# One-core linear attention and two gated feed-forward layers: loop attention placed between the front products, one block's exponentials per head, gate halves on one engine

## The chip, the cores and the metric

The kernel runs on one core of one Trainium2 chip. The metric is the device time of one execution in microseconds, as the median of several runs. PE is the matrix engine, DVE the vector engine, ACT the scalar (activation) engine, POOL the GpSimd engine, SP the engine that issues the DMAs.

## What is computed

Attention without a score matrix, then two feed-forward layers, all in float32:

```python
# q, k, v: (8, 8, 576, 64)
q_s = softmax of q over the 64 head columns
k_s = softmax of k over the 576 positions
x = q_s @ (k_s^T @ v)                  # laid out as 4608 tokens x 512
x = ((sigmoid(x @ w_gate) * (x @ w_val)) @ w_out)       # 512 -> 1536 -> 512
h = x @ w_in                                            # 512 -> 2048
g = (a0 + a1*h + a2*h^2 + a3*h^3) / (1 + |b0|*|h| + |b1|*h^2 + 1e-6)
out = g @ w_out2                                        # 2048 -> 512
```

## The kernel before

Every large product is made of three matmuls of split operands: each float32 value is cut into a high half (rounded to the matmul's format, copied by ACT) and a low half (value minus high half, on DVE or POOL). `mm3` (L168 to L171) multiplies high by high, low by high and high by low. Weights arrive as 64-bit numbers and are turned into float32 by four DVE operations on their bits (`prep_bits_a`, `prep_bits_b`, L203 to L218) before they are split.

The 4608 tokens are worked off in 9 blocks `j` of 512. In the first layer a block has 12 steps `f` (one per 128 columns of the 1536). A step is: the front products `pg` and `pv` (`front_a`, 4 pieces `kk` of 6 matmuls each, 24 in all), the sigmoid of `pg` on ACT, its product with `pv` on DVE, the split of that gate into `gh` and `gl` (`vec_a`), and the back products of the step before (`back_a`, 12 matmuls). The tiles `pg` and `pv` of a step fill the pool `ps_f`, so the next step's `pg` waits for this step's sigmoid and its `pv` for this step's gate product.

Attention is done in units `(j, u)`, one per block and pair of heads. For k: the column maximum (`att_km`), a transpose `ps_kt`, a maximum `mx` and a copy on DVE, a transpose back `ps_kb`, a copy `kma` on ACT (`att_kt`, `att_kb`), a subtraction on POOL (`att_ks`), an exponential on ACT (`att_ke`), the product `ps_kv` with v. For q: maximum, subtraction, exponential, sum, reciprocal and product (`att_qm`, `att_qs`, `att_qe`, `att_n`), four transposes `ps_qt` (`att_q`). The last product `ps_xt` gives a piece of x (`att_d`). All of these PE results go through the two banks of the pool `ps_x`, in turn.

The order of the work has two regimes. Block 0 with the attention of blocks 0 and 1 and all weights of the first layer is ordered by a planner (`in_time`, L59 on): a table of costs per kind of operation (`KINDS`) decides which operation is issued next and, for kinds with two engines, whether it goes to DVE or POOL (`Chosen`, recorded at L472). From block 1 on, a loop (L606 to L632) issues the steps, and the attention of block `j` runs during block `j - 1`: unit `u` has a due step `d`, and its parts are issued at `d - 5` to `d`. Before the change a step issues them in three places: `early_work` (the transpose `ps_kt`) right after the front products, `work` beside the gate's split, and `late_work` (`ps_kb`, the k subtraction) after the back products. In the same loop `prep` converts the weights of the second layer and stores them in DRAM. Engines run their instructions in issue order.

The second layer (144 steps of a front product `ph`, some DVE and ACT work and a back product `accb`) follows, and the diff leaves it alone.

Of the kernel before, what the change touches and what calls it, by code (L numbers as in the profile page):

```python
# [10 lines left out]
F32 = mybir.dt.float32  # L11
# [8 lines left out]
P = 128  # L20
# [23 lines left out]
    "q_max": (DVE, 0.68), "q_sub": ({DVE: 0.7, POOL: 1.05},), "q_exp": (ACT, 0.63, "exp"),  # L44
# [7 lines left out]
    "front": (PE, 1.37), "sig": (ACT, 0.6, "sigmoid"), "gate": (DVE, 0.7), "g_h": (ACT, 0.63),  # L52
    "g_l": ({DVE: 0.7, POOL: 1.29},),
    "back": (PE, 2.73), "next_h": (ACT, 0.62), "next_l": ({DVE: 0.7, POOL: 1.29},),
# [64 lines left out]
def kernel(ctx: ExitStack, tc: tile.TileContext, q, k, v, w1, w2, ab_in, out):  # L119
# [15 lines left out]
    def f32(ap):  # L135
        return ap.bitcast(F32)
# [6 lines left out]
    exp_bias = const.tile([P, 1], F32, name="exp_bias")  # L143
    q_one = 1.0 + 1e-6
# [77 lines left out]
    def prep_split(p, eng=nc.gpsimd):  # L222
        if p < NW1:
            wt[p] = [wpool.tile([P, NB], F32R, tag="w", name=n) for n in ("wh", "wl")]
            yield from split_steps(*wt[p], val.pop(p), eng)
        else:
            hl = stage.tile([P, 2, NB], F32R, tag="raw", name="hl")
            yield from split_steps(hl[:, 0], hl[:, 1], val.pop(p), nc.gpsimd)
            yield
            nc.sync.dma_start(out=w2_d[p - NW1], in_=f32(hl))  # L230
# [6 lines left out]
    def prep(stage_of):  # L237

        for p, n in stage_of:
            yield from (prep_load, prep_abs, prep_bits_a, prep_bits_b, prep_split)[n](p) or ()  # L240
            yield
# [25 lines left out]
    kt, vt, qt, kmt, qm = {}, {}, {}, {}, {}  # L267
# [14 lines left out]
    def heads(t):  # L282
        return t.rearrange("p c (h d) -> p (c h) d", d=D)
# [25 lines left out]
    def att_qm(j, u):  # L309
        qm[j, u] = att.tile([P, 8], F32, tag="qm", name="qm", bufs=4)  # L310
        nc.vector.tensor_reduce(out=qm[j, u], in_=heads(qt[j, u]), axis=AX.X, op=ALU.max)
# [6 lines left out]
    def att_qe(j, u):  # L318
        nc.scalar.activation(qt[j, u], qt[j, u], AF.Exp)

# [8 lines left out]
    def att_n(j, u, eng):  # L329
        g = heads(qt[j, u])  # L330
        t = att.tile([P, 8], F32, tag="qs", name="qs")
        nc.vector.tensor_reduce(out=t, in_=g, axis=AX.X, op=ALU.add)
        yield
        nc.vector.tensor_scalar(out=t, in0=t, scalar1=1e-9, scalar2=None, op0=ALU.add)
# [116 lines left out]
    def op(name, emit, *after):  # L451
        ops[name] = emit, [a for a in after if a]
# [22 lines left out]
    for i in range(2 * NHP):  # L475
        j, u = divmod(i, NHP)

        def n(what, back=0):
            return (what, *divmod(i - back, NHP)) if i >= back else None
# [11 lines left out]
        op(n("q_max"), partial(att_qm, j, u), n("load_q"), n("q_max", 1), n("q_sub", 3))  # L491
        op(n("q_sub"), partial(att_qs, j, u, Chosen(n("q_sub"))), n("q_max"))
        op(n("q_exp"), partial(att_qe, j, u), n("q_sub"))
        op(n("k_exp"), partial(att_ke, j, u), n("k_sub"), j and n("q_exp"))
        chain([n("q_sum"), n("q_add"), n("q_inv"), n("q_div")], att_n(j, u, Chosen(n("q_div"))), n("q_exp"), n("q_sum", 1), n("q_div", 2))
# [65 lines left out]
    work, early_work, late_work = {}, {}, {}  # L561

    def at(step, fn, *args):
        work.setdefault(max(step, NF1), []).append((fn, args))

    for j in range(2, NBLK):
        for u in range(NHP):
            d = NF1 * (j - 1) + UNIT_STEPS[u]
            if (j, u) != (2, 0):
                at(d - 5, load_k, j, u) if j < B else None  # L570
                at(d - 5, load_q, j, u)
# [12 lines left out]
            at(d - 1, att_q, j, u)  # L584
            at(d, att_d, j, u)
# [11 lines left out]

    prep_at = {}
    for p in range(NW1, NW):
        at0 = NF1 + 2 + 5 * (p - NW1) // 2  # L600
        for n, step in enumerate((0, 1, 1, 2, 2)):
            prep_at.setdefault(at0 + step, []).append((p, n))
# [176 lines left out]
```

## Time and profile before

| what | value |
|---|---|
| median of 3 runs | 1834.7 us (1833.99 to 1836.22) |
| the profiled execution, its own time | 1834.72 us |
| its span, first to last instruction | 1832.9 us |
| mean granted PE clock | 0.992 of full speed |
| PE, DVE, ACT, POOL busy, share of the span | 97%, 65%, 55%, 20% |
| HBM read, written | 92.44 MB, 35.65 MB |

The busy share is an average. PE's idle time lies in the first 850 us of the span; what it waits for there differs between the planned block and the loop, so they are read apart. A time in a row is in microseconds from the span's start unless it is a mean in ns.

### The profile page before, as it was taken

The numbers are of one execution on the slowest core, as the hardware profiler recorded it, in microseconds if no ns is written. First come the engines' busy times: TensorE is split into PE (matmuls) and PEld (weight loads), VectorE is DVE, ScalarE is ACT, GpSimd is POOL, SyncE is SP. The second block draws the span as 40 slices with busy tenths as digits, with TensorE's granted clock in tenths as the row PEclk, the third lists the DMA queues.
The fourth block names the chain that finished last, engine by engine and source line by source line (L and its number), as shares of the span: only waits on it lengthen the run. The fifth ranks groups of instructions, "written<-read, shape, count | busy, mean of one in ns | idle before, by whom it ended". The sixth has DMA issues, their size and how long they took to land.

```text
span 1832.9 us, 22295 instructions
## 1 busy us (share of the span) xinstructions
PE 1772.1 (97%) x8384; PEld 1452.7 (79%) x8384; DVE 1182.3 (65%) x1925; ACT 1005.6 (55%) x1652; POOL 363.3 (20%) x279
## 2 busy tenths in 40 slices
PE   5988999999999999999999999999999999999999
PEld 3766787787888878778888888888888888888887
DVE  9998545445455454454430288888888888887876
ACT  4556443444435354443331387777676777777765
POOL 3543010101011010110001122222222222222222
PEclk7999999999999999999999999999999999999999
DMA  6442323223132321312226401010000000000000
GB/s 206 146 150 89 115 68 107 69 64 114 62 123 75 110 79 54 123 61 84 78 77 212 160 24 43 5 47 12 35 23 24 24 24 24 23 24 24 1 24 23
DMA packets 53388, 129.54 MB, mean 71 GB/s; under 512 B 5664, under 2 KB 5664, under 8 KB 53280
## 3 DMA queue, kind: packets, MB, share of 16 engines
q1 hardware_dynamic: 53280, 128.12, 21.0%
q8 instruction: 66, 1.08, 0.2%
q14 instruction: 42, 0.34, 0.1%
HBM read 92.44 MB, written 35.65 MB: 70 GB/s over the span
## 4 chain that ended last, share of the span: by engine, by line
PE 56%; DVE 0%; ACT 0%; issue 0%
PE accb L698 21%; PE ph L171 7%; PE ph L170 7%; PE ph L169 7%; PE acc L430 4%; PE pg L169 1%; PE pv L169 1%; PE pg L171 1%; PE pv L171 1%; PE pg L170 1%; PE pv L170 1%; PE ps_qt L372 0%; PE ps_xt L170 0%; PE ps_xt L169 0%; PE ps_xt L171 0%; DVE km L287 0%
## 5 line engine op out<-in xcount | busy, mean ns | idle before, releaser
L415 DVE TENSOR_TENSOR sg<-pv,sg 128x512 f32<-128x512 f32 x108 | 74.4, 689 | 375.7 <-ACT sg L413 208.1
L162 POOL TENSOR_TENSOR glb<-gb,ghb 128x512 fp32r<-128x512 f32 x144 | 187.3, 1301 | 604.1 <-ACT ghb L160 585.4
L413 ACT ACTIVATE sg<-pg 128x512 f32<-128x512 f32 x108 | 64.5, 597 | 388.8 <-PE pg L171 387.0
L666 ACT ACTIVATE h<-ph 128x512 f32<-128x512 f32 x144 | 86.1, 598 | 196.9 <-PE ph L171 196.8
L169 PE MATMUL pg<-x_h,wh 128*128 128x512 f32 x432 | 172.1, 398 | 1.9 <-ACT sg L413 1.9
L169 PE MATMUL pv<-x_h,wh 128*128 128x512 f32 x432 | 169.3, 392 | 2.0 <-DVE sg L415 2.0
L170 PE MATMUL pv<-x_h,wl 128*128 128x512 f32 x432 | 168.9, 391 | 0.3 <-DVE wl L472 0.3
L171 PE MATMUL pv<-x_l,wh 128*128 128x512 f32 x432 | 168.9, 391 | 0.0
L170 PE MATMUL pg<-x_h,wl 128*128 128x512 f32 x432 | 168.8, 391 | 0.0
L171 PE MATMUL pg<-x_l,wh 128*128 128x512 f32 x432 | 168.7, 391 | 0.0
L698 PE MATMUL accb<-wh,ghb 128*128 128x512 f32 x576 | 158.3, 389 | 0.0
L698 PE MATMUL accb<-wl,ghb 128*128 128x512 f32 x576 | 158.3, 389 | 0.0
L698 PE MATMUL accb<-wh,glb 128*128 128x512 f32 x576 | 158.3, 389 | 0.0
L669 DVE SCALAR_TENSOR_TENSOR ah<-h,babs,ah 128x512 f32<-128x512 f32 x144 | 107.9, 750 | 54.5 <-ACT ah L667 54.5
L162 POOL TENSOR_TENSOR hl<-val,hl 128x512 fp32r<-128x512 f32 x32 | 41.3, 1290 | 475.1 <-ACT hl L160 224.3
L430 PE MATMUL acc<-gh,wl 128*128 128x512 f32 x432 | 122.4, 395 | 5.0 <-POOL wl L472 5.0
L430 PE MATMUL acc<-gh,wh 128*128 128x512 f32 x432 | 125.9, 402 | 0.4 <-DVE x_raw L436 0.3
L698 PEld LDWEIGHTS accb<-wl,ghb 128*128 128x128 f32 x576 | 108.1, 188 | 22.5
L698 PEld LDWEIGHTS accb<-wh,glb 128*128 128x128 f32 x576 | 108.1, 188 | 22.4
L698 PEld LDWEIGHTS accb<-wh,ghb 128*128 128x128 f32 x576 | 108.1, 188 | 22.4
L685 DVE SCALAR_TENSOR_TENSOR u<-ah,r 128x512 f32<-128x512 f32 x144 | 99.3, 690 | 39.5 <-ACT r L675 39.5
L169 PE MATMUL ph<-x_h,wh 128*128 128x512 f32 x320 | 124.5, 389 | 0.0
(129 smaller groups left out, 3974.5 us busy)
## 6 DMA issues: line engine op xcount, KB each, us to landing
raw<-in_w SPq DMA_DIRECT2D x68, 512.0 KB, 4.6
w<-hl SPq DMA_DIRECT2D x32, 512.0 KB, 2.9
v<-in_v SPq DMA_DIRECT2D x30, 325.0 KB, 3.3
k<-in_k SPq DMA_DIRECT2D x30, 320.0 KB, 4.1
q<-in_q SPq DMA_DIRECT2D x36, 256.0 KB, 4.2
x<-x_raw SPq DMA_DIRECT2D x36, 256.0 KB, 2.3
x_raw<-x SPq DMA_DIRECT2D x9, 1024.0 KB, 5.4
out<-ob SPq DMA_DIRECT2D x36, 256.0 KB, 2.3
```

Of the source, the lines that this page charges most:

```text
L162: lo_eng.tensor_tensor(out=lo, in0=src, in1=f32(h), op=ALU.subtract)
L169: nc.tensor.matmul(ps, wh, xh, start=first, stop=False)
L170: nc.tensor.matmul(ps, wl, xh, start=False, stop=False)
L171: nc.tensor.matmul(ps, wh, xl, start=False, stop=last)
L413: nc.scalar.activation(sg, pg, AF.Sigmoid)
L415: nc.vector.tensor_tensor(out=sg, in0=pv, in1=sg, op=ALU.mult)
L430: nc.tensor.matmul(accs["a", j][m], x[:, m * P:(m + 1) * P], y, start=(f == 0 and n == 0), stop=(f == NF1 - 1 and n == 2))
L666: nc.scalar.activation(h2, ph, AF.Square)
L669: nc.vector.scalar_tensor_tensor(out=ah, in0=h2, scalar=babs[:, 1:2], in1=ah, op0=ALU.mult, op1=ALU.add)
L685: nc.vector.scalar_tensor_tensor(out=u, in0=ah, scalar=q_one, in1=r, op0=ALU.add, op1=ALU.mult)
L698: nc.tensor.matmul(accs["b", j][t], x[:, t * P:(t + 1) * P], y, start=(f == 0 and n == 0), stop=(f == NF2 - 1 and n == 2))
```

## The change

1. **Loop attention.** The three lists of a step become one, keyed by step and by the piece `kk` of the front products after which the work is issued. `ps_kt`, `mx` and the copy come after piece 0 of step `d - 3`, `ps_kb`, `kma` and the k subtraction after piece 1, `ps_kv` and `ps_qt` after piece 2 of step `d - 1`, `ps_xt` after piece 0 of step `d`. The q exponential moves from step `d - 2` (next to the k exponential) to step `d - 3`, the q maximum and subtraction from `d - 4` to `d - 3`.
2. **Block 1's q exponential** (in the planned part) is done per head on ACT: eight activations of 128x64 that take the negated maximum as bias and write the row sums. Its subtraction and its sum on DVE or POOL fall away.
3. **Low halves.** In the planner's table `g_l` and `next_l` are DVE only.
4. The constant 1e-9 of the q sum comes from a tile `eps`; the store of a converted weight is issued one step after its split.

```diff
-    "q_max": (DVE, 0.68), "q_sub": ({DVE: 0.7, POOL: 1.05},), "q_exp": (ACT, 0.63, "exp"),
+    "q_max": (DVE, 0.68), "q_sub": ({DVE: 0.7, POOL: 1.05},), "q_exp": (ACT, 0.63, "exp"), "q_exps": (ACT, 2.1, "exp"),
...
-    "g_l": ({DVE: 0.7, POOL: 1.29},),
-    "back": (PE, 2.73), "next_h": (ACT, 0.62), "next_l": ({DVE: 0.7, POOL: 1.29},),
+    "front": (PE, 1.37), "sig": (ACT, 0.6, "sigmoid"), "gate": (DVE, 0.7), "g_h": (ACT, 0.63), "g_l": (DVE, 0.7),
+    "back": (PE, 2.73), "next_h": (ACT, 0.62), "next_l": (DVE, 0.7),
...
-            nc.sync.dma_start(out=w2_d[p - NW1], in_=f32(hl))
+            val[p] = hl
+
+    def prep_store(p):
+        nc.sync.dma_start(out=w2_d[p - NW1], in_=f32(val.pop(p)))
...
+    def att_qf(j, u):
+        g, m = heads(qt[j, u]), qm.pop((j, u))
+        qs[j, u] = att.tile([P, 8], F32, tag="qs", name="qs")
+        for i in range(8):
+            s = slice(i, i + 1)
+            nc.scalar.activation(g[:, i, :], g[:, i, :], AF.Exp, bias=m[:, s], accum_out=qs[j, u][:, s])
+            if i % 4 == 3:
+                yield
...
-                at(d - 4, att_km, j, u)
-                early_work.setdefault(max(d - 3, NF1 + 1), []).append((att_kt, (j, u, ps_x, "x")))
-                late_work.setdefault(max(d - 3, NF1 + 1), []).append((att_kb, (j, u, ps_x, "x")))
-                late_work[max(d - 3, NF1 + 1)].append((att_ks, (j, u, nc.gpsimd)))
-                at(d - 2, att_ke, j, u)
-                at(d - 3, load_v, j, u)
-                at(d - 1, att_kv, j, u)
-            at(d - 4, att_qm, j, u)
-            at(d - 4, att_qs, j, u, nc.vector)
-            at(d - 2, att_qe, j, u)
-            at(d - 2, att_n, j, u, nc.vector)
-            at(d - 1, att_q, j, u)
-            at(d, att_d, j, u)
+                at(d - 4, 1, att_km, j, u)
+                at(d - 3, 0, att_kt, j, u, ps_x, "x")
+                at(d - 3, 1, att_kb, j, u, ps_x, "x")
+                at(d - 3, 1, att_ks, j, u, nc.gpsimd)
+                at(d - 3, 2, load_v, j, u)
+                at(d - 2, 0, att_ke, j, u)
+                at(d - 1, 2, att_kv, j, u)
+            at(d - 3, 0, att_qm, j, u)
+            at(d - 3, 0, att_qs, j, u, nc.vector)
+            at(d - 3, 1, att_qe, j, u)
+            at(d - 2, 0, att_n, j, u, nc.vector)
+            at(d - 1, 2, att_q, j, u)
+            at(d, 0, att_d, j, u)
...
         for kk in range(KC):
             front_a(f, kk, *ps)
+            run(sequence((), work.get((i, kk), [])))
...
-        run(sequence((), early_work.get(i, [])))
-        run(prep(prep_at.get(i, [])), sequence(vec, work.get(i, [])))
+        run(vec, prep(prep_at.get(i, [])))
         if pend:
             back_a(*pend.pop(0))
-        run(sequence((), late_work.get(i, [])))
```

How the order moves at three places that the prediction speaks of.

PE, in a loop step of kind `d - 3` (the first unit of a block; `ps_kt` and `ps_kb` are the two transposes, `acc` the back products, `pg` and `pv` the front products). Before:

```order
L171 MATMUL pv<-x_l,wh 128x512
L293 MATMUL ps_kt<-ident,km 128x128
L430 MATMUL acc<-gh,wh 128x512 x4
L430 MATMUL acc<-gh,wl 128x512 x4
L430 MATMUL acc<-gl,wh 128x512 x4
L303 MATMUL ps_kb<-ident,km 128x128
```

and with the change:

```order
L172 MATMUL pv<-x_l,wh 128x512
L296 MATMUL ps_kt<-ident,km 128x128
L170 MATMUL pg<-x_h,wh 128x512
L171 MATMUL pg<-x_h,wl 128x512
L172 MATMUL pg<-x_l,wh 128x512
L170 MATMUL pv<-x_h,wh 128x512
L171 MATMUL pv<-x_h,wl 128x512
L172 MATMUL pv<-x_l,wh 128x512
L306 MATMUL ps_kb<-ident,km 128x128
```

The pair of transposes has moved from the two ends of the back products into the front products, six matmuls apart.

ACT, in a loop step that has the k transposes of one unit and the products of the unit before it (`kvh` and `qh` are the copies of `ps_kv` and `ps_qt`, `sg` the sigmoid, `gh` the gate's high half, ACT_TABLE_LOAD the change between the tables of exponential and sigmoid). Before:

```order
L413 ACTIVATE sg<-pg 128x512
L160 ACTIVATE gh<-sg 128x512
L360 ACTIVATE kvh_93<-ps_kv,rs 64x64 x2
L377 ACTIVATE qh<-ps_qt 128x512
L306 ACTIVATE kma<-ps_kb 128x128
```

and with the change:

```order
L309 ACTIVATE kma<-ps_kb 128x128
L322 ACT_TABLE_LOAD
L322 ACTIVATE q<-q 128x512
L375 ACTIVATE kvh_95<-ps_kv,rs 64x64 x2
L392 ACTIVATE qh<-ps_qt 128x512
L428 ACT_TABLE_LOAD
L428 ACTIVATE sg<-pg 128x512
L161 ACTIVATE gh<-sg 128x512
```

The step's sigmoid now stands behind a q exponential, two table loads and the copies of the attention products. Over the whole program the table loads go from 67 to 119.

POOL, in the planned block (`wl` are low halves of weights, `gl` of gates, `q` and `k` subtractions and products of the attention). A middle piece before:

```order
L472 TENSOR_TENSOR q<-q,qm 128x512
L472 TENSOR_TENSOR gl<-sg,gh 128x512
L472 TENSOR_TENSOR wl<-early,wh 128x512
L472 TENSOR_TENSOR gl<-sg,gh 128x512
L472 TENSOR_TENSOR wl<-early,wh 128x512 x2
L472 TENSOR_TENSOR gl<-sg,gh 128x512
```

and with the change:

```order
L487 TENSOR_TENSOR wl<-early,wh 128x512
L487 TENSOR_TENSOR q<-q,qs 128x512
L487 TENSOR_TENSOR wl<-early,wh 128x512 x13
L487 TENSOR_TENSOR q<-q,qs 128x512
L487 TENSOR_TENSOR k<-k,kma 128x640
```

In the planned block POOL's operations go from 46 to 33: `gl` 10 to 0, `wl` 23 to 20, the q subtraction 5 to 3, the k subtraction 6 to 5, the q product 2 to 5. On DVE `gl` goes from 2 to 12, `wl` from 13 to 16, the k subtraction from 2 to 3, the q subtraction from 3 to 1, the q product from 6 to 3, the q sum from 8 to 4.

## Rows read from the trace of the kernel before

**Rows 1.** Busy time by stage: stretch, length, busy us and count per engine, clock, DMA.

```profile
50.00:175.00 125.00, 106.53 (x511) 82.31 (x509) 119.06 (x194) 73.53 (x124) 65.25 (x36) 0.96 0.42 136
175.00:850.00 675.00, 658.25 (x3394) 539.55 (x3393) 326.68 (x634) 285.29 (x484) 74.03 (x52) 1.00 0.26 86
850.00:1800.00 950.00, 950.00 (x4199) 786.43 (x4198) 670.27 (x979) 606.74 (x975) 199.78 (x154) 1.00 0.13 45
```

**Rows 2.** Waits of PE from 175 to 850 us: total us, times, longest.

```profile
PE ps_qt L372 <- DVE mx L296: 12.3, 18, 1.1
PE ps_kb L303 <- DVE kvl L364: 3.7, 7, 1.2
```

**Rows 3.** PE in order of time in one loop step: start, us, what [idle before].

```profile
315.96 0.33 PE L293 MATMUL ps_kt<-ident,km 128*128 128x128 f32 x1
316.22 0.80 PE L348 MATMUL ps_kv<-v,k 128*64 128x65 f32 x20
318.17 0.63 PE L372 MATMUL ps_qt<-ident,q 128*128 128x128 f32 x4 [1.15 <-DVE mx L296]
...
322.76 0.30 PE L303 MATMUL ps_kb<-ident,km 128*128 128x128 f32 x1 [1.19 <-DVE kvl L364]
```

**Rows 4.** DVE in order of time in the same step.

```profile
317.15 0.68 DVE L415 TENSOR_TENSOR sg<-pv,sg 128x512 f32<-128x512 f32 x1
317.75 0.28 DVE L296 TENSOR_REDUCE mx<-ps_kt 128x1 f32<-128x128 f32 x1
318.06 0.23 DVE L298 COPY km<-mx 128x128 f32<-128x128 f32 x1
```

**Rows 5.** DVE in order of time in the planned block.

```profile
107.75 1.78 DVE L218 SCALAR_TENSOR_TENSOR early<-raw,early 128x512 uint32<-128x512 uint32 x1
```

**Rows 6.** POOL in order of time at the same place.

```profile
107.30 1.68 POOL L472 TENSOR_TENSOR gl<-sg,gh 128x512 fp32r<-128x512 f32 x1 [1.90 <-ACT gh L160]
```

**Rows 7.** Groups by line: `early` planned block, `val` loop; xcount, busy us, mean ns, idle.

```profile
L215 DVE SCALAR_TENSOR_TENSOR early<-raw,early 128x512 uint32<-128x512 uint32 x34 | 31.8, 935 | 0.0
...
L218 DVE SCALAR_TENSOR_TENSOR early<-raw,early 128x512 uint32<-128x512 uint32 x34 | 30.5, 898 | 0.0
...
L218 DVE SCALAR_TENSOR_TENSOR val<-raw,val 128x512 uint32<-128x512 uint32 x34 | 23.5, 692 | 1.1
L215 DVE SCALAR_TENSOR_TENSOR val<-raw,val 128x512 uint32<-128x512 uint32 x34 | 23.2, 683 | 0.0
...
L205 DVE TENSOR_SCALAR early<-early 128x512 f32<-128x512 f32 x34 | 20.6, 613 | 0.3 <-ACT early L199 0.2
...
L208 DVE TENSOR_SCALAR early<-early 128x512 uint32<-128x512 uint32 x34 | 19.8, 582 | 0.0
...
L208 DVE TENSOR_SCALAR val<-val 128x512 uint32<-128x512 uint32 x34 | 15.7, 462 | 0.1
L205 DVE TENSOR_SCALAR val<-val 128x512 f32<-128x512 f32 x34 | 14.5, 427 | 11.8 <-ACT val L199 11.6
```

**Rows 8.** Line L472 (operations with an engine chosen by the planner) by stage.

```profile
0.00:175.00 175.00, 21.80 (x28) 79.67 (x46) 0.91 0.47 154
```

**Rows 9.** Group by line of ACT: the table loads that precede a sigmoid.

```profile
L413 ACT ACT_TABLE_LOAD x33 | 42.3, 1283 | 5.5 <-PE pg L171 4.9
```

**Rows 10.** ACT in order of time in two loop steps.

```profile
331.69 1.28 ACT L327 ACT_TABLE_LOAD   x1
332.99 0.74 ACT L327 ACTIVATE k<-k 128x640 f32<-128x640 f32 x1
333.63 0.61 ACT L319 ACTIVATE q<-q 128x512 f32<-128x512 f32 x1
334.26 1.28 ACT L413 ACT_TABLE_LOAD   x1
...
341.00 0.63 ACT L360 ACTIVATE kvh<-ps_kv,rs 64x64 fp32r<-64x64 f32 x2 [1.09 <-DVE rs L355]
341.66 0.60 ACT L377 ACTIVATE qh<-ps_qt 128x512 fp32r<-128x512 f32 x1
```

More of the change, by code (lines that the diff above doesn't have):

```diff
@@ L51 @@
     "w_h": (ACT, 0.62), "w_l": ({DVE: 0.7, POOL: 1.29},),
-    "front": (PE, 1.37), "sig": (ACT, 0.6, "sigmoid"), "gate": (DVE, 0.7), "g_h": (ACT, 0.63),
-    "g_l": ({DVE: 0.7, POOL: 1.29},),
-    "back": (PE, 2.73), "next_h": (ACT, 0.62), "next_l": ({DVE: 0.7, POOL: 1.29},),
+    "front": (PE, 1.37), "sig": (ACT, 0.6, "sigmoid"), "gate": (DVE, 0.7), "g_h": (ACT, 0.63), "g_l": (DVE, 0.7),
+    "back": (PE, 2.73), "next_h": (ACT, 0.62), "next_l": (DVE, 0.7),
 }
@@ L143 @@
     exp_bias = const.tile([P, 1], F32, name="exp_bias")
+    eps = const.tile([P, 8], F32, name="eps")
+    nc.vector.memset(eps, 1e-9)
     q_one = 1.0 + 1e-6
@@ L228, in prep_split @@
             yield from split_steps(hl[:, 0], hl[:, 1], val.pop(p), nc.gpsimd)
-            yield
-            nc.sync.dma_start(out=w2_d[p - NW1], in_=f32(hl))
+            val[p] = hl
+    def prep_store(p):
+        nc.sync.dma_start(out=w2_d[p - NW1], in_=f32(val.pop(p)))
     def fetch(p):
@@ L239, in prep @@
         for p, n in stage_of:
-            yield from (prep_load, prep_abs, prep_bits_a, prep_bits_b, prep_split)[n](p) or ()
+            yield from (prep_load, prep_abs, prep_bits_a, prep_bits_b, prep_split, prep_store)[n](p) or ()
             yield
@@ L266 @@
     att = att_ctx.enter_context(tc.tile_pool(name="att", bufs=2))
-    kt, vt, qt, kmt, qm = {}, {}, {}, {}, {}
+    kt, vt, qt, kmt, qm, qs = {}, {}, {}, {}, {}, {}
     def load_k(j, u):
@@ L307, in att_kb, with att_qm @@
         yield
-    def att_qm(j, u):
+    def att_qm(j, u, negate=False):
         qm[j, u] = att.tile([P, 8], F32, tag="qm", name="qm", bufs=4)
-        nc.vector.tensor_reduce(out=qm[j, u], in_=heads(qt[j, u]), axis=AX.X, op=ALU.max)
+        nc.vector.tensor_reduce(out=qm[j, u], in_=heads(qt[j, u]), axis=AX.X, op=ALU.max, negate=negate)
     def att_qs(j, u, eng):
@@ L330, in att_n @@
         g = heads(qt[j, u])
[L331 to L334, printed above, removed]
+        t = qs.pop((j, u), None)
+        if t is None:
+            t = att.tile([P, 8], F32, tag="qs", name="qs")
+            nc.vector.tensor_reduce(out=t, in_=g, axis=AX.X, op=ALU.add)
+            yield
+        nc.vector.tensor_tensor(out=t, in0=t, in1=eps, op=ALU.add)
         yield
@@ L490 @@
         op(n("k_sub"), partial(att_ks, j, u, Chosen(n("k_sub"))), n("k_cp"))
-        op(n("q_max"), partial(att_qm, j, u), n("load_q"), n("q_max", 1), n("q_sub", 3))
-        op(n("q_sub"), partial(att_qs, j, u, Chosen(n("q_sub"))), n("q_max"))
-        op(n("q_exp"), partial(att_qe, j, u), n("q_sub"))
+        op(n("q_max"), partial(att_qm, j, u, j == 1), n("load_q"), n("q_max", 1), n("q_exp", 3))
+        if j == 0:
+            op(n("q_sub"), partial(att_qs, j, u, Chosen(n("q_sub"))), n("q_max"))
+            op(n("q_exp"), partial(att_qe, j, u), n("q_sub"))
+        else:
+            op(n("q_exps"), lambda g=att_qf(j, u): next(g), n("q_max"), n("q_div", 2), n("q_exp", 1))
+            op(n("q_exp"), ops[n("q_exps")][0], n("q_exps"))
         op(n("k_exp"), partial(att_ke, j, u), n("k_sub"), j and n("q_exp"))
-        chain([n("q_sum"), n("q_add"), n("q_inv"), n("q_div")], att_n(j, u, Chosen(n("q_div"))), n("q_exp"), n("q_sum", 1), n("q_div", 2))
+        chain(([] if j else [n("q_sum")]) + [n("q_add"), n("q_inv"), n("q_div")],
+              att_n(j, u, Chosen(n("q_div"))), n("q_exp"), n("q_add", 1), n("q_div", 2))
         chain([n("kv"), n("kv_add"), n("kv_inv"), n("kv_h"), n("kv_l")], att_kv(j, u), n("k_exp"), n("load_v"))
@@ L559, with at @@
         ops[o][0]()
-    work, early_work, late_work = {}, {}, {}
-    def at(step, fn, *args):
-        work.setdefault(max(step, NF1), []).append((fn, args))
+    work = {}
+    def at(step, kk, fn, *args):
+        work.setdefault((step, kk) if step >= NF1 else (NF1, 0), []).append((fn, args))
     for j in range(2, NBLK):
@@ L569 @@
             if (j, u) != (2, 0):
[L570 to L571 removed]
+                at(d - 5, 2, load_k, j, u) if j < B else None
+                at(d - 5, 2, load_q, j, u)
             if j < B:
[L573 to L585 removed]
+                at(d - 4, 1, att_km, j, u)
[11 more added lines that the diff above has]
+            at(d, 0, att_d, j, u)
     def split_x():
@@ L600 @@
         at0 = NF1 + 2 + 5 * (p - NW1) // 2
-        for n, step in enumerate((0, 1, 1, 2, 2)):
+        for n, step in enumerate((0, 1, 1, 2, 2, 3)):
             prep_at.setdefault(at0 + step, []).append((p, n))
```

## The prediction, made before the changed kernel was run

> **What bounds the kernel now.** I read the busy time by stage first [rows 1]. From 850 to 1800 us PE is busy for the whole 950 us: the second layer, which the change doesn't touch, and nothing can be won there. 950 us for 4199 matmuls is 0.226 us each, the pace of PE when it never waits. Two stages remain. In the loop (175 to 850 us) PE is busy 658.25 of 675 us, so 16.75 us idle. In the planned block it is DVE that is full: from 50 to 175 us DVE works 119.06 of 125 us, PE 106.53, ACT 73.53 [rows 1]. A gain has to come from one of these two: from PE's waits in the loop, or from DVE's work in the planned block.
>
> The waits of PE in the loop are two [rows 2]: 12.3 us in 18 waits of `ps_qt` for the reduction `mx`, and 3.7 us in 7 waits of `ps_kb` for `kvl`. One step shows the first [rows 3]: `ps_kt` starts at 315.96, `ps_kv` follows, and `ps_qt`, which needs the bank of `ps_kt`, waits 1.15 us. DVE reads that bank late [rows 4]: `mx` comes after the gate product of the step, which starts at 317.15, so it starts at 317.75. The back products are queued behind that `ps_qt` on PE. The second wait is the mirror image: `ps_kb` stands after the back products and needs the bank of `ps_kv`, which `kvl` leaves late (1.19 us). Neither is a shortage of an engine: DVE works 326.68 of the 675 us. PE waits because four users of two banks stand close together and DVE reaches them behind other work.
>
> **The change, part by part.**
>
> *The loop.* Now six front matmuls (6 x 0.226 = 1.36 us) stand between `ps_kt` and `ps_kb`, six more before `ps_kv` and `ps_qt`, and the bank of `ps_kt` has been read long before. `mx` and the copy take 0.28 + 0.23 us [rows 4], with 0.33 us of `ps_kt` before them [rows 3] and some 0.1 us of handing on (`mx` ends at 318.03, `ps_qt` starts at 318.17) about 0.95 us, under the 1.36 us of cover. In issue order `mx` now has ahead of it only the previous step's gate work, which falls into that step's back products (12 x 0.226 = 2.71 us) and the first piece. So both waits should go: 16.0 us [rows 2], and 16.75 us as the bound of what is idle. Against it: where `ps_kt`, `ps_kv` and `ps_qt` were one group, they are now two. The small matmuls take 0.26 us from `ps_kt` to the next start against 0.226 for a full product [rows 3], so one more break per unit costs PE at most some 0.1 us, 24 units 2.4 us, at least nothing. I take **-15 us**. The bound on the gainful side is -18: the idle time and 1.25 us from transposes that now overlap products. On the other side it is -8, half of the waits replaced by new ones.
>
> The price of the move lies on ACT. The q exponential had shared a table with the k exponential of the same step: load, k, q, load [rows 10]. One step earlier it needs its own pair of loads: 24 units x 2 loads x 1.283 us [rows 9] = 62 us more on ACT, which is busy 285.29 of 675 us [rows 1]. That is 2.6 us more in a step of nearly 10 us. I cost it at nothing because ACT waits for PE there; if that cover goes, the sigmoid is late, and next step's `pg` on PE with it. I work the slack out in the second rival.
>
> The k loads keep their step but the maximum that reads them comes earlier in its step; the weight stores leave their old place, where SP stood waiting for POOL with the next loads queued behind, so SP is relieved. Both beside other work: nothing.
>
> *The planned block.* DVE gains 10 gate halves, 3 weight halves and one k subtraction, and loses 2 q subtractions, 3 q products and 4 q sums. At 0.68 us for 128x512, as the gate product [rows 4], the k subtraction 640/512 of it, that is (10 + 3 + 1.25 - 2 - 3 - 4) x 0.68 = **+3.6 us**. That looks like a loss, since DVE is the full engine. But POOL's operations are not free for DVE. [rows 5] and [rows 6] show a DVE operation of 1.78 us while POOL's operation runs from 107.30 to 108.98; the same line takes 0.69 us in the loop [rows 7]. The four bit operations average 935, 898, 613 and 582 ns in the planned block against 683, 692, 427 and 462 ns in the loop [rows 7]: 0.76 us per weight, 34 weights, 26 us. POOL issues 46 operations there [rows 8], so 0.57 us of DVE each. The change takes 13 of them away: -7.4 us. The balance is 3.6 - 7.4 = -3.8 us. I take **-4 us**, as DVE is the full engine and PE stands in its shadow. The bounds: if each of the 13 had cost the full 1.78 - 0.68 = 1.10 us, -14.3 + 3.6 = -10.7; if the remaining 33 block DVE as often as the 46 did, +3.6.
>
> The Trainium skill, page "SBUF — State Buffer", section "SBUF: two separate sides", says that DVE and GpSimd share one port pair under an exclusive lock, held for a whole instruction, and that a DVE operation with two SBUF inputs is among those that block. By that rule every POOL operation that meets such work costs its full length, and the sum would go to the -10.7 end; the trace's average of 0.57 us says that about half of them meet it.
>
> The per-head exponentials replace 4 activations of 0.61 us [rows 10] by 32 small ones. No row shows one with row sums. The nearest from below is a `kvh` copy of 64 columns with a per-partition scalar, 0.31 us (two take 0.63 [rows 10]); from above, the whole exponential, 0.61. So +7.5 to +17 us of ACT, and four table loads more in this stage, 5.1 us. ACT goes from 73.53 to between 86 and 96 of the 125 us: not yet full, so nothing, which holds as long as DVE is the later one.
>
> The constant `eps` and the halves `next_l` (on DVE before too) change nothing.
>
> **The sum.** -15 - 4 = -19 us. The profiled execution took 1834.72 us (span 1832.9 and 1.8 around it), the median is 1834.7, so the sum goes straight onto it: **1815.7 us**.
>
> **The rivals.**
>
> *The planned block does not get shorter.* Were DVE blocked as often as before, or the planner's new order worse, the +3.6 us stays: 1834.7 - 15 + 3.6 = 1823.3. For it: what blocks DVE is when a POOL operation falls, and ACT's 12 to 22 us more can hold up a weight copy that DVE waits for. Against it: 13 fewer operations are certain. Chance 0.20.
>
> *The sigmoid comes late (slower).* In a step with `ps_kv`, count from its start. `ps_kv` 0.80 [rows 3], DVE's sum and reciprocal with their handing on some 0.4 (an estimate: the small DVE copy takes 0.23 [rows 4]), the two `kvh` 0.63, `qh` 0.60 [rows 10], the load 1.28, the sigmoid 0.60: it ends about 4.5 us after. PE goes through `ps_kv` and `ps_qt` (0.80 + 0.39), six front matmuls (1.36) and twelve back matmuls (2.71): it wants the bank of `pg` at 5.27. The slack is 0.8 us. It holds if the q exponential is done before `kvh`; if that waits for DVE's q subtraction and falls, with its load, behind (1.28 + 0.61 = 1.89 us), the sigmoid ends at 6.4, and PE waits 1.1 us in each of 24 steps: 27 us. Then 1834.7 - 19 + 27 = 1842.7. It decides at 0.8 us of lateness. Against it: the q subtraction comes three DVE operations after `ps_kt`, a whole piece and more ahead. Chance 0.08.
>
> The Trainium skill, page "ScalarE: Activation LUTs", sections "What ACT_TABLE_LOAD costs" and "Table sets: the hidden batching unit", speaks against this part of the change: batch by table, since a switch costs 1283 ns of load and about 1380 ns of drain. By that figure the sigmoid would end 1.38 us later, 0.6 us past the slack, an estimate of 15 us over 24 steps and 1830 us in all; the trace differs, as the k exponential starts 0.02 us after its load ends and the load 0.02 us after the q exponential ends [rows 10].
>
> *The transposes wait for each other.* If a POOL operation holds DVE's copy by 1.10 us, `ps_kb` is due 0.95 + 1.10 - 1.36 = 0.7 us too late; in every second unit, 12 x 0.7 = 8 us: 1834.7 - 19 + 8 = 1823.7. For it: POOL's split of the second layer's weights falls near the start of a step. Chance 0.12.
>
> **How the numbers follow.** The forecast, both parts within their bounds, has 0.55; the three rivals 0.20, 0.08 and 0.12; a larger gain than both bounds allow 0.05. The low end is near both full gains, -18 and -10.7: 1806. The high end takes in both cases at 1823 to 1824 and the loop at -8 with the block at +3.6, 1830: I set 1829, and leave out the slow rival and the tails. A change under 0.2% (3.7 us) can't be told from none; only the slow rival and mixtures of the others lie there or above: faster 0.88, same 0.05, slower 0.07.
>
> **What would show it.** Right: from the end of the planned block to about 850 us PE has under 4 us idle, and `ps_qt` no longer waits for `mx`; DVE's bit operations in the planned block average under 870 and 560 ns, and the first front product of block 1 starts some 4 us earlier; 119 table loads. Wrong: waits of `pg` for `sg` or of `ps_kb` for the copy in the loop; PE waits for ACT in the planned block; or the second layer taking another time.

## The result

The changed kernel takes **1810.7 us** (median of 4 runs, 1807.6 to 1812.3) against 1835.1 us of the kernel before (1834.0 to 1836.2): ratio 0.9865, 95% interval 0.9848 to 0.9882, faster by 24.4 us. The prediction was 1815.7 us with a range of 1806 to 1829. The profiled execution of the changed kernel took 1812.3 us, its span 1810.5 us, 22.4 us less than the span before; it is the slowest of the four. (Of the runs below, one execution of the kernel with the weights' low halves on DVE took 2020.7 us at a granted clock of 0.83 and is left out of its median.)

Where the 22.4 us are is read from the first front product of block 1 and the first of the second layer. The planned block ended at 174.40 us before and at 171.85 us now: -2.5. That is one execution of each. The same two orders of the planned block also ran in kernels of the experiments below: the old one ended at 175.05 and 176.53 us there, the changed one at 170.10, 170.21, 170.66 and 171.25 us. The means, 175.3 and 170.8, differ by 4.5 us; with the loop's 20.1 that is the 24.4 us of the medians. The loop, busy time by stage (columns as in [rows 1]), before:

```profile
174.40:1042.94 868.54, 851.79 (x4253) 699.60 (x4253) 379.56 (x720) 340.44 (x568) 93.30 (x67) 1.00 0.29 96
```

and after:

```profile
171.85:1020.33 848.48, 848.48 (x4253) 699.06 (x4253) 391.48 (x720) 407.13 (x615) 95.39 (x67) 1.00 0.29 98
```

PE issues the same 4253 recorded matmuls and no longer stands still: the loop is 20.1 us shorter, and no wait of PE is listed in it. 16.75 of these were idle time before; the other 3.3 are PE's busy time, 851.79 to 848.48. ACT has 66.7 us more to do. The second layer took 790.0 us before and 790.2 now.

The stages of [rows 1], after:

```profile
50.00:175.00 125.00, 110.69 (x533) 85.64 (x532) 118.77 (x207) 89.12 (x192) 41.14 (x23) 0.96 0.43 141
175.00:850.00 675.00, 675.00 (x3484) 555.74 (x3483) 347.37 (x649) 359.57 (x542) 76.98 (x53) 1.00 0.27 89
850.00:1800.00 950.00, 950.00 (x4198) 786.46 (x4197) 677.00 (x985) 612.98 (x986) 204.45 (x157) 1.00 0.12 43
```

In the planned block DVE is as full as it was (118.77 of 125 us against 119.06), ACT has 15.6 us more, POOL 24 us less. The loop step that answers to [rows 3], PE in order of time:

```profile
306.30 0.27 PE L296 MATMUL ps_kt<-ident,km 128*128 128x128 f32 x1
...
307.79 0.27 PE L306 MATMUL ps_kb<-ident,km 128*128 128x128 f32 x1
...
309.37 0.80 PE L363 MATMUL ps_kv<-v,k 128*64 128x65 f32 x20
310.11 0.66 PE L387 MATMUL ps_qt<-ident,q 128*128 128x128 f32 x4
...
314.73 0.39 PE L170 MATMUL pg<-x_h,wh 128*128 128x512 f32 x1
```

None of the four starts after an idle time (it would stand in brackets at the row's end). ACT in the same step, as [rows 10]:

```profile
308.40 1.28 ACT L322 ACT_TABLE_LOAD   x1
309.69 0.63 ACT L322 ACTIVATE q<-q 128x512 f32<-128x512 f32 x1
310.67 0.63 ACT L375 ACTIVATE kvh<-ps_kv,rs 64x64 fp32r<-64x64 f32 x2 [0.35 <-DVE rs L370]
311.33 0.60 ACT L392 ACTIVATE qh<-ps_qt 128x512 fp32r<-128x512 f32 x1
311.95 1.28 ACT L428 ACT_TABLE_LOAD   x1
313.24 0.60 ACT L428 ACTIVATE sg<-pg 128x512 f32<-128x512 f32 x1
```

The sigmoid ends at 313.84, 4.47 us after `ps_kv` starts, and PE takes the bank at 314.73, 5.36 us after: a slack of 0.89 us, where the prediction had worked out 4.5, 5.27 and 0.8.

The bit operations of the planned block, as [rows 7] (the four of `val` in the loop now average 685, 682, 427 and 421 ns):

```profile
L219 DVE SCALAR_TENSOR_TENSOR early<-raw,early 128x512 uint32<-128x512 uint32 x34 | 29.7, 873 | 0.0
L216 DVE SCALAR_TENSOR_TENSOR early<-raw,early 128x512 uint32<-128x512 uint32 x34 | 29.0, 856 | 0.0
...
L209 DVE TENSOR_SCALAR early<-early 128x512 uint32<-128x512 uint32 x34 | 18.9, 560 | 0.0
L206 DVE TENSOR_SCALAR early<-early 128x512 f32<-128x512 f32 x34 | 16.1, 488 | 0.4 <-ACT early L200 0.4
```

Their excess over the loop's is now (2777 - 2215) ns x 34 = 19.1 us, for 33 operations of POOL 0.58 us each, against 26 us and 0.57 before.

### The profile page after: what moved, and what is told of

Read it like the earlier page. It is cut to its first block, busy times and chain, and to the rows that moved or that the text cites. A ratio compares the mean times of both kernels' runs of the same rounds, so it can differ in the third digit from the quotient of the medians.

```text
span 1810.5 us, 22332 instructions
## 1 busy us (share of the span) xinstructions
PE 1767.9 (98%) x8384; PEld 1451.5 (80%) x8384; DVE 1190.3 (66%) x1931; ACT 1085.7 (60%) x1764; POOL 340.0 (19%) x266
## 4 chain that ended last, share of the span: by engine, by line
PE 91%; DVE 5%; ACT 1%; issue 1%; DMA 0%; SPq 0%; DVEq 0%; ACTq 0%
PE accb L721 22%; PE acc L445 15%; PE ph L170 7%; PE ph L171 7%; PE ph L172 7%; PE pg L170 5%; PE pg L171 5%; PE pg L172 5%; PE pv L170 5%; PE pv L172 5%; PE pv L171 5%; DVE early L216 1%; PE ps_kv L363 1%; PE ps_qt L387 1%; DVE early L219 1%
## 5 line engine op out<-in xcount | busy, mean ns | idle before, releaser
L170 PE MATMUL pg<-x_h,wh 128*128 128x512 f32 x432 | 177.2, 410 | 3.3 <-ACT sg L428 3.3
L721 PEld LDWEIGHTS accb<-wh,glb 128*128 128x128 f32 x576 | 108.1, 188 | 22.4
L721 PEld LDWEIGHTS accb<-wh,ghb 128*128 128x128 f32 x576 | 108.2, 188 | 22.4
L171 PE MATMUL ph<-x_h,wl 128*128 128x512 f32 x320 | 124.5, 389 | 0.0
L172 PE MATMUL ph<-x_l,wh 128*128 128x512 f32 x320 | 124.5, 389 | 0.0
```

What stands on the lines that cost most here:

```text
L170: nc.tensor.matmul(ps, wh, xh, start=first, stop=False)
L171: nc.tensor.matmul(ps, wl, xh, start=False, stop=False)
L172: nc.tensor.matmul(ps, wh, xl, start=False, stop=last)
L721: nc.tensor.matmul(accs["b", j][t], x[:, t * P:(t + 1) * P], y, start=(f == 0 and n == 0), stop=(f == NF2 - 1 and n == 2))
```

## The experiments

In all of them the theory is the prediction's: two waits of PE in the loop, a DVE that is the bound of the planned block and pays for POOL's operations, and ACT beside other work in both. Times are medians; the kernel before had 1834.4 to 1835.3 us beside them.

**The two parts apart.** First the loop alone: the planned block's table of costs and its q operations as before.

```diff
-    "g_h": (ACT, 0.63), "g_l": (DVE, 0.7),
-    "next_h": (ACT, 0.62), "next_l": (DVE, 0.7),
+    "g_h": (ACT, 0.63), "g_l": ({DVE: 0.7, POOL: 1.29},),
+    "next_h": (ACT, 0.62), "next_l": ({DVE: 0.7, POOL: 1.29},),
...
-        op(n("q_max"), partial(att_qm, j, u, j == 1), n("load_q"), n("q_max", 1), n("q_exp", 3))
-        if j == 0:
+        op(n("q_max"), partial(att_qm, j, u), n("load_q"), n("q_max", 1), n("q_sub", 3))
+        if True:
...
```

> The loop as in the changed kernel, the planned block as in the kernel before. If the gain comes from the two banks of ps_x in the loop (the traces: the stage from block 1 to the second layer went from 868.5 to 848.45 us), this kernel takes 1835 - 20 = 1815 us, its planned block ends at the old 174.4 us, and PE has under 1 us of waits from 175 to 850 us. Rival, the loop is shorter because the planned block hands over a different state (buffers, weights loaded further ahead): then the loop stage stays above 855 us and the time above 1820 us.

Measured: 1815.6 us (ratio 0.9895, 0.9882 to 0.9909). The block ends at 175.05 us, the loop takes 848.42 us. The loop's part is this, whatever the planned block hands over.

Then the planned block alone, with the loop of the kernel before (its three lists, its places and its weight store).

```diff
-    work = {}
-    def at(step, kk, fn, *args):
-        work.setdefault((step, kk) if step >= NF1 else (NF1, 0), []).append((fn, args))
+    work, early_work, late_work = {}, {}, {}
+    def at(step, fn, *args):
+        work.setdefault(max(step, NF1), []).append((fn, args))
...
```

> The planned block as in the changed kernel, the loop and the place of the weight stores as in the kernel before. If the two parts add up, the time is 1835 - 2.5 to - 4.5 = 1830.5 to 1832.5 us, the first front product of block 1 starts at about 171.9 us instead of 174.4, and the loop stage keeps its 868.5 us with the 16 us of waits of PE. Rival, the planned block gives nothing by itself (the 2.55 us are a difference of starts that the loop would have swallowed): 1834 to 1836 us.

Measured: 1831.05 us over 9 runs (ratio 0.9978, 0.9969 to 0.9988). The block ends at 170.10 us. The loop's gain of 19 us and this one of 3 us add up to the change, within some 2 us.

**The block's two halves.** The low halves and the per-head exponentials were undone one at a time: the first by the `if j == 0` part of the diff above alone, the second by its table part alone.

> The changed kernel with block 1's q exponential whole again (subtraction, one exponential, sum by an operation), the low halves still on DVE only. The planner then puts 4 q sums, one q subtraction and 4 q products more on DVE, and 5 weight halves and one k subtraction less; POOL gets 5 weight halves, 3 q subtractions and one k subtraction more and 4 q products less, 5 operations more. If DVE sets the end of the planned block and a POOL operation costs DVE 0.57 us, DVE gets (9 - 5 - 1.25) x 0.68 + 5 x 0.57 = 4.7 us more: 1810.7 + 4.7 = 1815.4 us, and the block ends near 176 us. Rival, ACT's 16.7 us of small exponentials and sum reads hold the block up as much as they spare DVE: then no change, or up to 3 us faster.

> The changed kernel with the planner free again to put the gates' low halves on POOL. It puts 6 of them there, and one q product goes from POOL to DVE: DVE has 5 operations of 0.68 us less, POOL 5 more. With 0.57 us of DVE per POOL operation the balance is (0.57 - 0.68) x 5 = -0.6 us: 1810 us, not to be told from the changed kernel. If each POOL operation costs DVE its 1.10 us: +2.1 us, 1812.8. If a POOL operation costs DVE nothing: -3.4 us, 1807.3; but a low half that comes from POOL is 1.3 us instead of 0.7 and the back product that waits for it is late, so a time above 1813 us would put the gain of the change on this chain and not on DVE's sum.

Measured: **1805.8 us** without the per-head exponentials (ratio 0.9843, 0.983 to 0.9856; the four runs from 1805.4 to 1806.7), 1818.2 us with the low halves free (0.9909, 0.9894 to 0.9924). Both central values fall, 1815.4 and 1810 us. Without the per-head exponentials the gain is larger than even the rival allowed; with the low halves free the time lies above 1813 us, which the expectation had given to late back products and not to DVE's sum. With the loop-only kernel the four make a square:

| median us (end of the planned block) | low halves on DVE or POOL | on DVE only |
|---|---|---|
| q exponential of block 1 whole | 1815.6 (175.05) | 1805.8 (165.75) |
| per head, with sums | 1818.2 (178.00) | 1810.7 (171.85) |

The low halves on DVE give 7.5 to 9.7 us; the per-head form costs 2.6 to 4.9 us. Busy time from the start to the end of the block, in the order top left, top right, bottom left, bottom right:

```profile
0.00:175.05 175.05, 133.90 (x664) 102.38 (x664) 164.53 (x287) 96.67 (x167) 83.14 (x68) 0.91 0.46 154
```

```profile
0.00:165.75 165.75, 130.61 (x664) 100.02 (x665) 158.21 (x294) 97.72 (x167) 76.09 (x60) 0.93 0.48 163
```

```profile
0.00:178.00 178.00, 134.89 (x665) 102.08 (x665) 163.87 (x287) 111.63 (x234) 65.05 (x60) 0.97 0.47 152
```

```profile
0.00:171.85 171.85, 133.22 (x665) 101.77 (x665) 160.46 (x292) 109.63 (x231) 57.32 (x55) 0.97 0.48 157
```

From the first row to the second DVE does 7 instructions more in 6.3 us less, and its idle time falls from 10.5 to 7.5 us. The four bit operations sum to 3031 ns in the one and 2704 ns in the other: 11.1 us over 34 weights, for 8 operations of POOL fewer, 1.4 us each. From the third row to the fourth the sums are 2910 and 2777 ns, 4.5 us for 5 operations fewer, 0.9 us each. That points to a gate's low half costing DVE more than the mean of 0.57 us, but it does not prove it, since the planner also moved other operations. The rival, that PE waits for what POOL delivers late, is not excluded either: from 36 us to the end of the block PE's waits for POOL fall from 8.3 to 3.4 us between the first two rows; between the other two they are 1.8 us in both, beside one of 5.2 us for a q product. From the second row to the fourth DVE's idle time grows from 7.5 to 11.4 us and ACT's work by 11.9 us. So the per-head form spares DVE no time in the end, and DVE waits more. The stretch with the most of ACT, without the per-head form:

```profile
60.00:80.00 20.00, 19.34 (x84) 15.29 (x84) 19.75 (x36) 12.78 (x21) 12.29 (x5) 1.00 0.53 185
```

and with it:

```profile
60.00:80.00 20.00, 18.85 (x75) 14.94 (x74) 19.06 (x35) 19.00 (x39) 3.48 (x2) 0.90 0.49 158
```

ACT is full there for 19 of 20 us, though it works only 89.12 of the 125 us of the stage. But DVE idles only 0.7 us more in it, of 3.9 us in the whole block; the rest is spread, most of it before 36 us and behind 140 us. So the full ACT of this stretch is not shown to be the loss. From 36 to 76 us the changed kernel has these waits of PE over 2 us (total us, times, longest):

```profile
PE ps_qt L387 <- POOL q L487: 5.2, 1, 5.2
PE ps_kt L296 <- DVE km L290: 3.8, 1, 3.8
```

The first takes the place of one of 4.7 us for DVE's q product in the kernel with whole exponentials, since the planner has put this product on POOL; the second has no counterpart there. The first front product starts at 40.81 us, at 39.10 with whole exponentials and at 37.83 in the kernel before.

**Is it ACT's time or the planner's order?** Two runs. One changes only the planner's price of the per-head piece (`"q_exps": (ACT, 2.1, "exp")` to 0.6), which gives another order of the same instructions.

> The changed kernel with one number changed: the planner's price of four per-head exponentials, 2.1 us, set to 0.6 us. The instructions are the same, their order in the planned block is another. The run without the per-head exponentials was 4.9 us faster. If that loss is ACT's time and its table loads, it stays, whatever the order: 1809 to 1813 us. If it is the order that the planner made of it (PE stood 3.8 us at 54.7 us of the span before a transpose whose maximum DVE reached late), another order moves the time by several us either way: under 1808 or over 1814 us.

Measured: 1810.3 us (0.9864, 0.9847 to 0.988): another order, the same time. It does not clear the order, though: the two waits of PE above are there again, with 5.2 and 3.0 us. The other keeps the order of the 1805.8 us kernel and adds nothing but time on ACT.

```diff
...
         nc.scalar.activation(qt[j, u], qt[j, u], AF.Exp)
+        if j == 1:
+            for i in range(10):
+                s = slice(i % 8, i % 8 + 1)
+                nc.scalar.activation(spare, ident[:, :56], AF.Exp, bias=eps[:, s], accum_out=spare_s[:, s])
...
```

> The kernel with block 1's q exponential whole again (1805.8 us), and behind each of the four exponentials ten spare ones of 56 columns with row sums on ACT (the output is not touched). Nothing moves on DVE, POOL or PE, whose order and choice of engine stay. At 0.33 us from one to the next that is 40 x 0.33 = 13.3 us of ACT, as much as the per-head form costs: 32 x 0.335 - 4 x 0.53 = 8.6 us and four table loads more, 5.1 us. If ACT's time is what made the per-head form 4.9 us slower, the time goes to 1810 or 1811 us. If it is what the planner made of the missing operations (another order, five q products on POOL instead of one), it stays at 1805 to 1807 us.

Measured: 1818.3 us (0.9909, 0.9894 to 0.9924), +12.4 us. The spare exponentials were dearer than assumed, 0.47 us from one to the next (below), 4 x 10 x 0.47 = 18.8 us of ACT; the loss is two thirds of that. One place in order of time on ACT:

```profile
161.59 0.63 ACT L323 ACTIVATE q<-q 128x512 f32<-128x512 f32 x1
162.13 0.33 ACT L327 ACTIVATE ab<-ident,eps 128x56 f32<-128x56 f32 x1
162.36 0.19 ACT L327 ACTIVATION_READ_ACCUMULATOR ab<-ident,eps 128x1 f32 x1
162.58 0.34 ACT L327 ACTIVATE ab<-ident,eps 128x56 f32<-128x56 f32 x1
...
166.75 0.72 ACT L345 ACTIVATE k<-k 128x640 f32<-128x640 f32 x1
```

and PE's waits from 150 to 179 us of the same kernel:

```profile
PE ps_kv L368 <- ACT k L345: 4.9, 1, 4.9
PE ps_xt L171 <- ACT kma L310: 4.4, 1, 4.4
```

PE stands for the k exponential behind the spare work. These two waits are 9.3 us, and from 150 to 179 us PE's granted clock was 0.76, against 0.97 in the kernel without the spare work, so a part of the 12.4 us is PE's lower pace. Added time on ACT can reach the end, then, though ACT works only 86.83 of the 125 us from 50 to 175. The changed kernel has neither of these two waits at its per-head exponentials, so its own loss need not come about in this way. How much of the per-head form's 4.9 us is ACT's time and how much the planner's other choice of engines was not separated.

**POOL's price once more.** The weights' low halves were put on DVE too (`"w_l": (DVE, 0.7)`), in the changed kernel and in the 1805.8 us one.

> The changed kernel with the weights' low halves on DVE only too: POOL loses 20 operations, DVE gets 20 x 0.68 = 13.6 us more. At the average price of 0.58 us of DVE per POOL operation that is +2 us: 1812 to 1813 us. The runs before have shown a higher price for the gates' halves: fitted to the excess of the bit operations in four kernels, about 1 us for a gate's low half and 0.5 us for another operation; by this +3.6 us, 1814 us. If each POOL operation cost 1.10 us: -8.4 us, 1802 us. Above 1818 us DVE alone is the bound, and POOL's operations cost it next to nothing.

> The q exponential whole again, and also the weights' low halves on DVE only: POOL loses 25 operations, DVE gets 25 x 0.68 = 17.0 us of them and gives four q products to POOL. The same step in the changed kernel cost 0.9 us for 20 operations, 0.63 us of DVE saved per POOL operation taken away. By that it is 1806 to 1808 us here. In this kernel the bit operations' excess is only 16.4 us for 38 operations of POOL, 0.43 us each: by that +3 to +6 us, 1809 to 1812 us. Under 1804 us it would be the best version.

Measured: in the changed kernel 1811.6 us (0.9867, 0.985 to 0.9883), no difference that can be told; in the other 1809.0 us (0.9856, 0.9839 to 0.9872), 3.2 us slower. 20 to 25 operations of 0.68 us more on DVE against as many of POOL fewer nearly cancel, as 0.57 us each says; for a weight's low half the 1.10 us price is out. It does not beat 1805.8 us.

**The loop: does `ps_kt` alone do it?** The kernel before with only `ps_kt` and the maximum behind it after the first piece.

```diff
         for kk in range(KC):
             front_a(f, kk, *ps)
+            if kk == 0:
+                run(sequence((), early_work.get(i, [])))
...
-        run(sequence((), early_work.get(i, [])))
```

> The kernel before with one thing moved: the transpose ps_kt, the maximum and the copy behind it, from after the front products to after their first piece. All else of the loop stays (ps_kb after the back products, the q exponential beside the k exponential, no more table loads). If the two waits are separate, the 12.3 us of ps_qt for mx go and the 3.7 us of ps_kb for kvl stay: 1834.4 - 12.3 = 1822 us, with up to 4 us less again if PE's idle after the breaks goes as well. Rival, the banks only change partners, and ps_qt now waits for the readers of ps_kv or ps_kv for the copy: less than half of it, above 1828 us. If it gives 20 us, to 1815 us, the rest of the loop's change, with its 52 table loads, was not needed.

Measured: **1924.6 us** (1.0484, 1.0468 to 1.0499), slower by 89. No expectation had this. The loop by time and PE's waits in it, from 176.53 us to the second layer (waits from 180 to 850 us):

```profile
176.53:1133.40 956.87, 889.18 (x4252) 720.20 (x4253) 380.14 (x720) 340.16 (x568) 93.33 (x67) 0.96 0.26 87
```

```profile
PE ps_kt L293 <- DVE km L287: 56.5, 17, 4.1
```

The waits of `ps_qt` are gone and a larger one has come: `ps_kt` needs the k maximum of the step before. DVE in order of time ahead of one such wait:

```profile
325.70 0.68 DVE L162 TENSOR_TENSOR gl<-sg,gh 128x512 fp32r<-128x512 f32 x1
327.73 0.69 DVE L332 TENSOR_REDUCE qs<-q 128x8 f32<-128x512 f32 x1 [1.34 <-ACT q L319]
...
330.52 1.22 DVE L287 TENSOR_REDUCE km<-k 128x128 f32<-128x640 f32 x1
331.66 0.68 DVE L311 TENSOR_REDUCE qm<-q 128x8 f32<-128x512 f32 x1
```

The maximum is issued at the end of step `d - 4`, behind a q sum that waits for ACT; in this step it ends at 331.74 us, after `ps_kt` had kept PE waiting for 4.06 us. In the kernel before that time passed under the front products. So the early transpose needs an earlier maximum. The changed kernel moves it from the end of step `d - 4` into the front products, and the next run shows that this is enough: there the q exponential, and the q sum with it, is back, and `ps_kt` has no wait. Whether the q exponential's move alone would also do was not run. And the loop is 88 us longer for 51 us more of idle (67.7 against 16.75): the other 37 us are PE's busy time, 889.18 against 851.79, at a granted clock of 0.96 in place of 1.00.

**The loop: was the q exponential's own place needed?** The changed kernel with it back beside the k exponential.

```diff
-            at(d - 3, 0, att_qm, j, u)
-            at(d - 3, 0, att_qs, j, u, nc.vector)
-            at(d - 3, 1, att_qe, j, u)
+            at(d - 4, 1, att_qm, j, u)
+            at(d - 4, 1, att_qs, j, u, nc.vector)
+            at(d - 2, 0, att_qe, j, u)
```

> The changed kernel with the loop's q exponential back beside the k exponential of step d - 2, and its maximum and subtraction back in step d - 4, behind the k maximum. It saves 52 table loads, 67 us of ACT. If ACT's loads lie beside other work, as predicted, nothing is won: 1810 to 1812 us. DVE's q sum now waits for an exponential of the same step, with the k maximum of the next unit and the gate product queued behind it; if the gate product comes late by it, pv waits for it on PE: 24 steps of up to 1 us, up to 1835 us. Faster than 1807 us would mean that the loads cost something after all.

Measured: 1824.9 us (0.9944, 0.9929 to 0.9959), 14.2 us slower than the changed kernel, with 48 table loads fewer in the loop (the other 4 are the planned block's). The loop takes 862.48 us. Its busy time and PE's waits from 180 to 1040 us:

```profile
170.66:1033.14 862.48, 854.33 (x4253) 697.16 (x4253) 380.36 (x720) 341.82 (x567) 93.08 (x67) 1.00 0.29 96
```

```profile
PE pv L170 <- DVE sg L430: 6.7, 12, 0.7
PE ps_kb L306 <- DVE km L301: 0.9, 4, 0.3
```

and DVE in one step of it:

```profile
321.52 0.69 DVE L347 TENSOR_REDUCE qs<-q 128x8 f32<-128x512 f32 x1 [4.68 <-ACT q L322]
...
323.29 1.30 DVE L290 TENSOR_REDUCE km<-k 128x128 f32<-128x640 f32 x1
...
325.22 0.69 DVE L318 TENSOR_TENSOR q<-q,qm 128x512 f32<-128x512 f32 x1
325.83 0.69 DVE L430 TENSOR_TENSOR sg<-pv,sg 128x512 f32<-128x512 f32 x1
```

The gate product waits behind the q sum, which waits for ACT. The listed waits are 7.6 us of the 14; PE's busy time is 5.9 us more, at a granted clock of 1.00. The 62 us of table loads are not a price that is merely covered: they buy a q exponential that is done a step before DVE wants it.

**The loop: the slack of the sigmoid.** The changed kernel with 12 spare copies on ACT ahead of the sigmoid's table load, in the 24 steps with `ps_kv`.

```diff
...
+        if any(fn is att_kv for fn, _ in work.get((i, 2), [])):
+            for _ in range(12):
+                nc.scalar.activation(spare, ident[:, :D], AF.Copy)
         vec = vec_a(j, f, *ps)
```

> The changed kernel with 12 spare copies of 64 columns on ACT, between the copies of ps_kv and ps_qt and the sigmoid's table load, in the 24 odd steps (the output is not touched). Their price is not in the trace; the nearest row, a copy of 64 columns with a scalar at 0.31 us alone and two in 0.63, is the upper end, so the sigmoid is 1.5 to 3.7 us later. In the trace of the changed kernel the sigmoid ends about 0.9 us before PE wants the bank of pg. If this slack is what decides, each of the 24 steps is longer by the lateness less 0.9 us: 0.6 to 2.8 us a step, +15 to +67 us, 1826 to 1878 us, as waits of pg for sg on PE. Rival, the pools give more room than the one bank (PE has other work to go on with): under +5 us.

Measured: 1884.9 us (1.0268, 1.0253 to 1.0284), +74 us. ACT in one step, and PE's waits from 171.25 us to the second layer at 1088.7:

```profile
322.58 3.44 ACT L639 ACTIVATE ab<-ident 128x64 f32<-128x64 f32 x12
326.04 1.28 ACT L429 ACT_TABLE_LOAD   x1
```

```profile
PE pg L171 <- ACT sg L429: 50.5, 24, 2.5
```

All 24 steps wait, 2.1 us each for 3.44 us of lateness: the slack is 0.9 to 1.3 us. The sigmoid's slack is real and as narrow as the slow rival had it. In the traces the loop is 69 us longer, of which 50.5 are waits; PE's busy time in it is 866.97 us in place of 848.48, its granted clock 0.99.

**The store.** The changed kernel with the weight store back in the step of its split (`enumerate((0, 1, 1, 2, 2))`, the store behind the split).

> The changed kernel with the weight stores back in their old place, in the step of the split, where SP stands for POOL's low half with the next loads queued behind it. If SP's wait lies beside other work, as predicted, the time stays at 1810 to 1812 us. If the k loads come late by it, the k maximum that is now wanted 1 to 2 us earlier in its step is late, and PE waits for it at ps_kt, as it did where ps_kt alone was moved (4.1 us in each unit): above 1815 us, up to 1900 us.

Measured: 1813.4 us (0.9883, 0.9868 to 0.9898), 2.7 us slower than the changed kernel; the loop takes 850.63 us, with one wait of PE:

```profile
PE ps_kb L304 <- DVE km L299: 2.0, 1, 2.0
```

So the new place of the store is worth some 2 us, and isn't what makes the loop.

## Why the prediction was right, point by point

- **The two waits of the loop.** The mechanism was right: both waits went, and the loop-only run shows that the loop's gain stands by itself. The term was too small, -15 us where -20 was measured, beyond even its bound of -18. The mis-sized step is "one more break per unit costs PE at most some 0.1 us", taken against the gain: with the small groups set apart PE's busy time fell by 3.3 us instead of rising by up to 2.4, and the bound had allowed it a fall of 1.25. Why it fell is not separated. In the run with the q exponential put back, where short waits of PE return, it rose by 5.9 us. This term is nearly all of the 5 us by which the forecast was too high.
- **The price on ACT in the loop at nothing.** Right, with the slack at 0.89 us against 0.8. (The terms that the prediction lists up to the sigmoid's end add up to 4.31 us, not 4.5; the trace has 4.47.) That it is a slack and no surplus is shown by the spare copies. What the prediction did not say is that the move was needed: with the q maximum, subtraction and exponential put back, it costs 14 us.
- **"The k loads keep their step but the maximum that reads them comes earlier in its step."** Named in half a sentence and costed at nothing. Where the early transpose came without it the kernel was 89 us slower. The weight store, also costed at nothing, is worth 2 us.
- **DVE in the planned block.** The sum was met: -4 was said, and the block is shorter by 2.5 us in the profiled pair, 4.5 us as the mean of all traces, and 3.3 us as the block-only run's median. The terms were near too: 33 operations of POOL at 0.58 us against 46 at 0.57, 6.9 us less excess where 7.4 was said. But that the sum came out is luck, by two errors that cancel. Split as the square splits it, the low halves alone should have brought 10 x (0.68 - 0.57) = 1.1 us more of work on DVE, and gave 7.5 to 9.7 us of time; the per-head form should have spared DVE 4.7 us, and cost 2.6 to 4.9. For the low halves the wrong step was one mean price for every operation of POOL, and no price for a half that comes late; the runs do not tell the two apart.
- **ACT in the planned block: "not yet full, so nothing".** The second wrong step: the per-head form is not free. The spare exponentials show that added time on ACT can reach the end, where it stands in the chain from the q exponential to the k exponential to `ps_kv`. Through which chain the per-head form itself loses its time stays open. The Trainium skill, page "ScalarE: Activation LUTs", section "Table sets: the hidden batching unit", asks to batch activations by table set. Against that rule the per-head form took four table loads more, 4 x 1.283 us, and was slower; but in the loop 48 loads more went with a kernel that is 14.2 us faster, and there the measurement decides against the rule.
- **The signs given ahead.** No wait of `ps_qt` for `mx` and 119 table loads came true. The bit operations are at their limits and not all under them (856 and 873 against 870, 488 and 560 against 560). "The first front product of block 1 some 4 us earlier" was 2.5 in this execution and 4.5 in the mean of the traces. PE's waits for ACT in the planned block, a sign of being wrong, are there, but the kernel before has them too.

## What to carry to other kernels

Before a transpose is moved forward, look up where its operand is made in the issue order of that engine, and what the engine waits for just before; here the operand had to move too. An engine with a third of its time idle is not always free, as the spare exponentials show: ask which instruction stands behind the added one and who waits for that, and measure the parts of a mixed change one by one, since here one half earned 9.7 us and the other gave 4.9 back. The best version of all runs is the changed kernel without the per-head exponentials: 1805.8 us.

## What was not expected of the hardware

An exponential with row sums is two instructions on ACT, all 32 of the changed kernel grouped:

```profile
L330 ACT ACTIVATE q<-q,qm 128x64 f32<-128x64 f32 x32 | 10.7, 335 | 0.3 <-DVE qm L314 0.2
L330 ACT ACTIVATION_READ_ACCUMULATOR q<-q,qm 128x1 f32 x32 | 6.0, 187 | 0.0
```

The reading of the sum takes 187 ns, and the next exponential starts 0.33 us after the one before it where each writes columns of its own (61.92, 62.26 and 62.59 us of the span), 0.47 us in the spare run, where all write the same columns. Whether the shared columns are the reason was not tested.

And waits of PE cost more than their length in three runs: PE's busy time for the same loop rose by 5.9 us at a granted clock of 1.00 (short waits, q exponential put back), and by 18 and 37 us at mean granted clocks of 0.99 and 0.96 where waits of 2 to 4 us recurred in 24 and 19 of the loop's 96 steps. The kernel with the early transpose shows the clock at work in one step:

```profile
326.44 0.39 PE L170 MATMUL pg<-x_h,wl 128*128 128x512 f32 x1
...
331.80 0.48 PE L293 MATMUL ps_kt<-ident,km 128*128 128x128 f32 x1 [4.06 <-DVE km L287]
...
332.50 0.63 PE L170 MATMUL pg<-x_h,wl 128*128 128x512 f32 x1
332.93 0.63 PE L171 MATMUL pg<-x_l,wh 128*128 128x512 f32 x1
```

Before the wait the granted clock was 1.00 and the products started 0.23 us apart; after it, from 333 to 336 us, it was 0.50, the lower of the two levels (1.2 GHz), and they start 0.43 us apart. After the wait of 2.46 us that the kernel with the spare copies shows at 327.99 us the clock stayed at 1.00.
